# Filter blocks of the convolution two per PE session, and their writes behind the first expert's F tiles

## The chip, the cores and the metric

The kernel runs on one core of a Trainium2 chip. The metric is the device time of one execution in microseconds (us). PE is TensorE, DVE is VectorE, ACT is ScalarE, POOL is GpSimd, SP is SyncE, which here only issues transfers.

## The reference

Two branches of the same 2048 x 512 input x are mixed row by row with a gate:

```python
g = sigmoid((x * gate_w).sum(-1, keepdims=True))
a = x * (long_conv(kv, ssm_k) + kv * ssm_D)    # kv = shift_conv(k) * v
b = top-2-of-8 mixture of experts: sum_e gate_e * ((silu(x@w_gate_e) * (x@w_up_e)) @ w_down_e)
return g * a + (1 - g) * b
```

The long convolution is over 2048 positions for each of 512 channels and is done by a discrete Fourier transform of length 4096, split into two stages for each of the inputs. The experts have F = 1376, that is 11 F tiles of up to 128 rows.

## The kernel before

**The experts.** Their order is found on the chip, the busiest first; each takes up to CAPS rows (568 for the first). `up(ft)` works on one F tile: it loads `raw` (512 KB, gate and up weights, three buffers) and `rd` (256 KB, down weights, two buffers) through SP, splits each into a rounded high part and a low part (`gh` and `dh` on ACT, `gl` and `dl` on DVE), and multiplies: for each half of the rows (h = 0 of 256 columns, h = 1 of 312 for the first expert) twelve matmuls into a PSUM tile `g` and twelve into `u`. These share three PSUM banks. ACT takes silu of `g` into `sg`, which frees the bank of `g`; DVE multiplies `sg` by `u`, which frees the bank of `u`; `hh` (ACT) and `hl` (DVE) split the result. `down` multiplies three or more F tiles' results by `dh`, `dl` into PSUM tiles `yp` (tag "y", three banks).

**The routing.** While the first expert runs, DVE also works out which rows go to the other experts: one-hot tables `hots`, then `vals`, and PE gathers them into lists with 32 small matmuls each (`list`). The rows of the next expert are then gathered by POOL (`xg`), turned on PE (`xgp`) and split into `xh` (ACT) and `xl` (DVE).

**The filter.** Its first stage takes 16 blocks of 128 rows (`ssk`), in the order 1 to 15 and then 0, through four matmuls of 64 rows by 128 columns in full float32 (`c1`); the result goes out to `kd` in device memory, 512 KB a block, and is read back by the filter's second stage (`x_stage2`), much later. The first ten blocks (ks1 to ks10) run in the opening stage, whose order is written out by hand. Their results wait in SBUF: ks2, ks4, ks6 in buffers "ev" (three), ks7 to ks10 in "B" (five), ks1, ks3, ks5 in "A" (six). Writes of ks2, ks4, ks6, ks7 and ks8 (`now`) are issued by POOL as soon as the first expert's last rows are split (anchor "act rest"); the nine other transfers (`rest_k`, which ends with a load of the constant `cr`) follow three per F tile from F tile K0 = 4 on, each behind the ACT split `gh` of that tile (anchor "gh 0 ft").

**The last six blocks** (ks11 to ks15 and ks0) are generators in the list `fill`. `tick()` starts the next entry and advances those that run; it is called in proportion to the F tiles done, `total * seen / n_up` with n_up = 88 * 0.97 = 85.4 and total = 75 entries. After the six filter blocks come the 16 blocks of the input's first stage (`x_stage1`), the 16 steps of the second stage (`x_stage2`) and the four of the last (`y_stage`). Pairs of blocks are loaded by `k_pair`, the first of them (`kr11`) still in the opening stage. Block 0 has the vector `dD` added by POOL. The tile scheduler then decides where in each engine's queue a step's instructions stand.

**A session.** A group of full float32 matmuls between the experts' matmuls is called a session here. `all_free` makes the first matmul of a session wait until the two PSUM banks of tag "m" and the three of tag "y" have been read, so that the rest need no wait.

Of the kernel before, what the change touches and what calls it, by code (L numbers as in the profile page):

```python
# [18 lines left out]
AF = mybir.ActivationFunctionType  # L19
# [11 lines left out]
PL = S // P  # L31
# [23 lines left out]
BUB = (1, 1, 3)  # L55
XG = 3
Z0, Z1 = (7, 6)
RM = 5
K0, LATE = (4, 3)
SEQ_N = 10  # L60
BUSY = (17, 1, 2, 1, 1)
VD = (1, 2, 3, 4, 5, 6)
# [78 lines left out]
def gated_mix(ctx: ExitStack, tc: tile.TileContext, a, out):  # L141
    nc = tc.nc
    sync, act, dve, pool, pe = nc.sync, nc.scalar, nc.vector, nc.gpsimd, nc.tensor
# [7 lines left out]
    kd = dram.tile([P, 2, PL, D], F32, name="kd")  # L151
# [24 lines left out]
    def banks(name):  # L176
        return ps.tile([P, 2 * D], F32, tag="m", bufs=1, name=name)

    def turned(name):
        return ps.tile([P, D], F32, tag="y", bufs=3, name=name)  # L180
# [4 lines left out]
    c1 = cp.tile([P, P], F32, name="c1")  # L185
# [6 lines left out]
    def two(tag, name):  # L192
        return fp.tile([P, 2 * D], F32, tag=tag, bufs={"B": BW, "ev": EV}[tag], name=name)

    def half(t, n):
        return t[:, n * D:(n + 1) * D]

    def split2(t):
        return t.rearrange("p (n d) -> p n d", n=2)
# [24 lines left out]
    def fetch(r, src):  # L224
        with after("sp"):
            d = sync.dma_start(r, src)

        return d

    def load(tag, bufs, name, src):  # L230
        r = t2k(tag, bufs, name)
        fetch(r, src)
        return r


    @contextmanager
    def behind(first):
        with tc.high_priority(), tc.issue_after(first):
            yield
# [9 lines left out]
    written = []  # L249
# [60 lines left out]
    kr = {}  # L310

    k_order = [*range(1, PL), 0]
# [12 lines left out]
    def k_out(pl, **how):  # L325
        return stage1_f32(kr[pl], kd, pl, f"ks{pl}", **how)

    def k_pair(n):
        pl, after_ = k_order[n:n + 2]
        if after_ == pl + 1:  # L330
            w = two("B", f"kr{pl}")
            d = fetch(split2(w), a["ssk"][pl * P:(pl + 2) * P].rearrange("(b p) d -> p b d", b=2))
            kr[pl], kr[after_] = half(w, 0), half(w, 1)
            return d
        k_load(pl)
        k_load(after_)

    def k_stage1(pl):
        n = k_order.index(pl)
        if n % 2 == 0 and pl not in kr:  # L340
            k_pair(n)
        yield
        yield
        k_out(pl)

    krows = {}

# [5 lines left out]
    def x_stage1(pl):  # L353
        if pl == 0:
            with after("sp"):
                sync.dma_start(sk, a["sk"].unsqueeze(0).to_broadcast([P, TAPS, D]))
        for r in range(-3, 1):
            krow(pl + r)
        v = load("T", 3, f"v{pl}", rows(a["v"], pl))
        yield  # L360
        acc = half(two("B", f"acc{pl}"), 0)
        tmp = t2k("T", 3, f"tmp{pl}")
        dve.tensor_mul(acc, krow(pl), sk[:, 0])
        for tap in range(1, TAPS):
            dve.tensor_mul(tmp, krow(pl - tap), sk[:, tap])
            dve.tensor_add(acc, acc, tmp)
        dve.tensor_mul(acc, acc, v)
        hl = pairs(acc, f"xs{pl}", (dve, dve))
        yield
        stage1(hl, xd, pl, f"xs{pl}")  # L370
# [8 lines left out]
    read_y = []  # L379

    def all_free(i, *ready):
        both_free(i)
        for f in (*read_y[-3:], *ready):
            tc.add_manual_dep(i, f.name, mybir.DependencyInfo(
                mybir.DependencyClass.Sync, mybir.DependencyReason.DATA), reason="all at once")
# [12 lines left out]
    def halves(p):  # L398
        return [half(p, n) for n in range(2)]
# [54 lines left out]
    def y_stage(pl):  # L454
# [13 lines left out]
        for n in (0, 2):  # L468
# [8 lines left out]
        yield  # L477

    wait = lambda n: [iter(()) for _ in range(n)]
    fill = ([k_stage1(i) for i in k_order[SEQ_N:]] + wait(BUB[0]) + [x_stage1(i) for i in range(PL)] + wait(BUB[1]) +  # L480
            [g for i in range(NK // 2) for g in (x_stage2(i), iter(()))] + wait(BUB[2]) +
            [g for i in range(0, PL, 4) for g in (y_stage(i), *wait(3))])
    fill.reverse()
# [11 lines left out]
    def after(engine):  # L495
        return nullcontext() if ordered or engine not in anchor else tc.issue_after(anchor[engine])


    def behind_rows(i, name="act rest"):
        tc.add_manual_dep(i, anchor[name].name, mybir.DependencyInfo(  # L500
            mybir.DependencyClass.Sync, mybir.DependencyReason.DATA), reason="behind the gather")
# [443 lines left out]
    for i in range(4):  # L945
        dve.tensor_tensor(hot0[:, i], u0[:, 4 * i:4 * i + 4].unsqueeze(1).to_broadcast([P, P, 4]), io4, op=ALU.is_equal)
        for j in range(4):
            n = 4 * i + j
# [24 lines left out]
    act.activation(sg0, key[:, :1], AF.Silu)  # L973
    behind_rows(first.load_down(0).ins, "act 1")
    behind_rows(first.load_down(1).ins, "act 1")
    behind_rows(k_pair(SEQ_N).ins, "act 1")
    behind_rows(first.load(2), "act 1")
    behind_rows(first.load(3), "act 1")
    evict8()
# [10 lines left out]
    first.product(0, 0, 1, between=last_rows)  # L990
    first.product(0, 1, 0, hi_first=True)
    first.split(1, act, dve)
    now = [f for f in written if f.home == "ev"] + [f for f in written if f.home == "B"][:2]
    for f in now:
        behind_rows(f.write().ins)
    rest_k = [f for f in written if f not in now]
    rest_k.append(SimpleNamespace(write=lambda: pool.dma_start(cr, a["c_r"])))
    order.close()
    ordered = False
# [156 lines left out]
    with tc.For_i(0, nb_v, 1) as b:  # L1156
        with tc.tile_pool(name="over", bufs=1) as op:
            e = nc.values_load(blk[0:1, ds(b, 1)], engines=(mybir.EngineType.SP,),
                               min_val=0, max_val=E - 1)
# [7 lines left out]
            p = turned("oxp").rearrange("p (k n) -> p k n", k=KT)  # L1167
# [5 lines left out]
            for ft, (f0, fw) in enumerate(FT):  # L1173
                n = 2 * KT * fw
# [68 lines left out]
```

## Time and profile before

| | us |
|---|---|
| median of three runs (945.50, 945.69, 954.07) | 945.69 |
| the profiled execution | 943.48 |
| span of its profile | 941.70 |
| outside the span (943.48 - 941.70) | 1.78 |
| PE busy, share of the span | 926.2, 98% |
| DVE busy, share of the span | 642.3, 68% |

A busy PE is not PE at its peak, because matmuls are pipelined and their ends are modelled: in the timeline the start of one matmul to the start of the next is the measure, and a step longer than the usual one shows what lies between. A timeline row has the start in us, the duration in us, engine, line, operation, out<-in, sizes, a count where equal rows are merged, and in brackets the idle time of that engine before it and what ended it. Lines 202 to 204 are the helper that records every expert matmul, so tiles are told apart by name and time.

### The profile page before, as it was taken

To read this page: it belongs to the slowest core of one execution; us is meant where nothing else is said; L and a number is where in the kernel's file an instruction comes from. 1 tells how busy PE (TensorE), PEld (TensorE's weight loads), DVE (VectorE), ACT (ScalarE), POOL (GpSimd) and SP (SyncE) were. 2 spreads that over 40 slices of the span, in tenths; PEclk is the share of its full clock that TensorE was granted. 3 is DMA by queue.
4 is the path that set the end of the run, shared out by engine and by line. 5 is a ranking of instruction groups with operands and counts; after the bars stand their busy time and mean duration, and the time that the engine had idled before them with its cause. 6 is when DMAs were issued, how large, how long until landed. Compare 5 with 4: busy or idle time off the path is not lost.

```text
span 941.7 us, 18495 instructions
## 1 busy us (share of the span) xinstructions
PE 926.2 (98%) x7117; PEld 832.4 (88%) x7117; DVE 642.3 (68%) x1190; ACT 510.2 (54%) x883; POOL 152.1 (16%) x137
## 2 busy tenths in 40 slices
PE   8999999999999999999999999999999999999996
PEld 4789999999999999978898889888887989889984
DVE  4797699999998556556767666765777645553541
ACT  4644344754456545478656876668766544234330
POOL 0333000310003020130101211013010310121012
PEclk9999999999999999999999999999999999999998
DMA  9996945764457463456445655356543786777233
GB/s 331 325 318 203 377 164 179 207 205 155 145 196 195 157 204 111 136 146 201 146 136 169 165 179 179 142 164 176 182 168 123 189 276 180 195 202 212 73 54 46
DMA packets 76381, 172.06 MB, mean 183 GB/s; under 512 B 8481, under 2 KB 9377, under 8 KB 76162
## 3 DMA queue, kind: packets, MB, share of 16 engines
q1 hardware_dynamic: 53490, 121.89, 38.3%
q0 software_dynamic: 12464, 29.02, 13.7%
q10 hardware_dynamic: 10336, 19.93, 5.7%
q8 instruction: 58, 0.95, 0.4%
q14 instruction: 33, 0.27, 0.1%
HBM read 127.24 MB, written 43.57 MB: 181 GB/s over the span
## 4 chain that ended last, share of the span: by engine, by line
PE 87%; issue 4%; ACT 3%; DVE 2%; DMA 2%; POOL 0%; SPq 0%; ACTq 0%; POOLq 0%; DVEq 0%
PE yp L202 9%; PE yp L204 9%; PE yp L203 9%; PE u L202 8%; PE u L203 8%; PE u L204 8%; PE g L202 8%; PE g L203 8%; PE g L204 8%; PE xgp L522 2%; PE zp L392 2%; PE yp L464 2%; PE x2p L392 1%; PE k2p L392 1%; PE yt L716 1%
## 5 line engine op out<-in xcount | busy, mean ns | idle before, releaser
L202 PE MATMUL u<-xh,gh 128*128 128x256 f32 (+14 forms) x704 | 202.6, 288 | 2.4 <-ACT sg L644 2.2
L203 PE MATMUL u<-xl,gh 128*128 128x256 f32 (+14 forms) x704 | 201.1, 286 | 0.0
L204 PE MATMUL u<-xh,gl 128*128 128x256 f32 (+14 forms) x704 | 201.1, 286 | 0.0
L202 PE MATMUL g<-xh,gh 128*128 128x256 f32 (+17 forms) x696 | 201.0, 289 | 0.0
L204 PE MATMUL g<-xh,gl 128*128 128x256 f32 (+17 forms) x696 | 198.9, 286 | 0.0
L203 PE MATMUL g<-xl,gh 128*128 128x256 f32 (+17 forms) x696 | 198.7, 285 | 0.0
L202 PEld LDWEIGHTS u<-xh,gh 128*128 128x128 f32 (+1 forms) x704 | 131.0, 186 | 6.1 <-ACT sg L644 3.0
L202 PEld LDWEIGHTS g<-xh,gh 128*128 128x128 f32 (+1 forms) x696 | 129.5, 186 | 7.7 <-DVE sg L645 1.6
L203 PEld LDWEIGHTS u<-xl,gh 128*128 128x128 f32 (+1 forms) x704 | 131.0, 186 | 3.5 <-issue 3.2
L204 PEld LDWEIGHTS g<-xh,gl 128*128 128x128 f32 (+1 forms) x696 | 129.5, 186 | 4.3 <-issue 4.1
L204 PEld LDWEIGHTS u<-xh,gl 128*128 128x128 f32 (+1 forms) x704 | 131.1, 186 | 0.9 <-issue 0.8
L203 PEld LDWEIGHTS g<-xl,gh 128*128 128x128 f32 (+1 forms) x696 | 129.5, 186 | 2.5 <-issue 0.8
L646 ACT ACTIVATE hh<-sg 128x256 fp32r<-128x256 f32 (+14 forms) x176 | 73.0, 418 | 103.2 <-DVE sg L645 101.5
L202 PE MATMUL yp<-hh,dh 128*128 128x264 f32 (+13 forms) x440 | 127.4, 290 | 0.0
L203 PE MATMUL yp<-hl,dh 128*128 128x264 f32 (+13 forms) x440 | 126.9, 288 | 0.0
L204 PE MATMUL yp<-hh,dl 128*128 128x264 f32 (+13 forms) x440 | 126.5, 288 | 0.0
L644 ACT ACTIVATE sg<-g 128x256 f32<-128x256 f32 (+14 forms) x176 | 68.1, 388 | 98.9 <-PE g L204 96.9
L592 DVE TENSOR_TENSOR gl<-raw,gh 128x1024 fp32r<-128x1024 f32 (+1 forms) x88 | 105.4, 1197 | 19.7 <-ACT gh L586 19.3
L645 DVE TENSOR_TENSOR sg<-sg,u 128x256 f32<-128x256 f32 (+14 forms) x176 | 74.8, 426 | 64.6 <-PE u L204 63.3
L586 ACT ACTIVATE gh<-raw 128x1024 fp32r<-128x1024 f32 (+1 forms) x88 | 91.4, 1038 | 49.2 <-PE u L203 47.5
L513 POOL DMA_INDIRECT xg<-in_q,gidx x37 | 43.9, 1187 | 304.4 <-PE xgp L522 254.0
L653 ACT ACTIVATE dh<-rd 128x512 fp32r<-128x512 f32 (+1 forms) x88 | 53.5, 628 | 71.4 <-PE yp L203 25.5
(289 smaller groups left out, 1609.5 us busy)
## 6 DMA issues: line engine op xcount, KB each, us to landing
raw<-in_wgu SPq DMA_DIRECT2D x80, 512.0 KB, 4.5
rd<-in_wd SPq DMA_DIRECT2D x80, 256.0 KB, 4.5
kl<-kd SPq DMA_DIRECT2D x16, 512.0 KB, 5.3
xl<-xd SPq DMA_DIRECT2D x32, 256.0 KB, 3.8
zd<-ze ACTq DMA_DIRECT2D x16, 512.0 KB, 4.7
zl<-zd SPq DMA_DIRECT2D x16, 512.0 KB, 5.6
out<-zt SPq DMA_DIRECT2D x21, 256.0 KB, 6.4
krow<-in_kpad SPq DMA_DIRECT2D x19, 256.0 KB, 4.4
```

The costliest lines, as they stand in the source:

```text
L202: pe.matmul(p, wh, hi, start=start, stop=False)
L203: pe.matmul(p, wh, lo, start=False, stop=False)
L204: return pe.matmul(p, wl, hi, start=False, stop=stop)
L392: i = pe.matmul(p[r][64 * c:64 * c + 64], w[64 * r:64 * r + 64, 64 * c:64 * c + 64], rows_(r, c)[64 * r:64 * r + 64], start=True, stop=Tru ...
L464: i = pe.matmul(p[b][64 * t:64 * t + 64], c2, half(r[b], t), start=True, stop=True).ins
L513: anchor["pool"] = pool.indirect_dma_start(out=xg[:w], out_offset=None, in_=a["q"], in_offset=bass.IndirectOffsetOnAxis(ap=gidx[:w, col:co ...
L586: anchor[f"gh {r} {ft}"] = act.activation(st["gh", ft], raw, AF.Copy).ins
L592: dve.tensor_sub(st["gl", ft][:, c], raw[:, c], st["gh", ft][:, c].bitcast(F32))
L644: act.activation(sg[:fw, :nn], pp[0][:fw, :nn], AF.Silu)
L645: dve.tensor_mul(sg[:fw, :nn], sg[:fw, :nn], pp[1][:fw, :nn])
L646: act.activation(hh[:fw, sl], sg[:fw, :nn], AF.Copy)
L653: act.activation(dh[:fw], rd[:fw], AF.Copy)
```

## The change

Three things are changed. First, `k_stage1` takes two blocks at a time: one generator loads the pair, and two ticks later one session of eight matmuls does both. The second block goes to two banks of tag "y", and ACT evicts it in two halves. Second, the pair of ks11 and ks12 is no longer loaded in the opening stage, and `fill` begins with K_WAIT = 3 empty entries; each session is followed by an empty one, so the list has 78 entries instead of 75 and `x_stage1` begins three entries later. Third, no write of a block is issued at once: the five that were go to the head of `rest_k`, which now has 14 entries and starts at F tile K0 = 2.

```diff
@@ -56,7 +56,7 @@
 XG = 3
 Z0, Z1 = (7, 6)
 RM = 5
-K0, LATE = (4, 3)
+K0, LATE, K_WAIT = (2, 3, 3)
 SEQ_N = 10
 BUSY = (17, 1, 2, 1, 1)
 VD = (1, 2, 3, 4, 5, 6)
@@ -335,13 +335,25 @@
         k_load(pl)
         k_load(after_)
 
-    def k_stage1(pl):
-        n = k_order.index(pl)
-        if n % 2 == 0 and pl not in kr:
-            k_pair(n)
+    def k_stage1(n):
+        k_pair(n)
         yield
         yield
-        k_out(pl)
+        pls = k_order[n:n + 2]
+        both, p1 = banks(f"ks{pls[0]}p"), [turned(f"ks{pls[1]}p{t}") for t in range(2)]
+        last = None
+        for p, pl in ((halves(both), pls[0]), (p1, pls[1])):
+            for t in (1, 0):
+                part = slice(64 * t, 64 * t + 64)
+                with after("pe") if last is None else behind(last):
+                    i = pe.matmul(p[t], c1[part], kr[pl][part], start=True, stop=True).ins
+                if last is None:
+                    all_free(i)
+                last = i
+        out1(both, kd, pls[0], f"ks{pls[0]}")
+        ev = two("ev", f"ks{pls[1]}e")
+        read_y.extend(act.activation(half(ev, t), p1[t], AF.Copy).ins for t in range(2))
+        act.dma_start(kd[:, :, pls[1], :], split2(ev))
 
     krows = {}
 
@@ -477,7 +489,7 @@
         yield
 
     wait = lambda n: [iter(()) for _ in range(n)]
-    fill = ([k_stage1(i) for i in k_order[SEQ_N:]] + wait(BUB[0]) + [x_stage1(i) for i in range(PL)] + wait(BUB[1]) +
+    fill = (wait(K_WAIT) + [g for n in range(SEQ_N, PL, 2) for g in (k_stage1(n), iter(()))] + wait(BUB[0]) + [x_stage1(i) for i in range(PL)] + wait(BUB[1]) +
             [g for i in range(NK // 2) for g in (x_stage2(i), iter(()))] + wait(BUB[2]) +
             [g for i in range(0, PL, 4) for g in (y_stage(i), *wait(3))])
     fill.reverse()
@@ -973,7 +985,6 @@
     act.activation(sg0, key[:, :1], AF.Silu)
     behind_rows(first.load_down(0).ins, "act 1")
     behind_rows(first.load_down(1).ins, "act 1")
-    behind_rows(k_pair(SEQ_N).ins, "act 1")
     behind_rows(first.load(2), "act 1")
     behind_rows(first.load(3), "act 1")
     evict8()
@@ -990,10 +1001,8 @@
     first.product(0, 0, 1, between=last_rows)
     first.product(0, 1, 0, hi_first=True)
     first.split(1, act, dve)
-    now = [f for f in written if f.home == "ev"] + [f for f in written if f.home == "B"][:2]
-    for f in now:
-        behind_rows(f.write().ins)
-    rest_k = [f for f in written if f not in now]
+    rest_k = [f for f in written if f.home == "ev"] + [f for f in written if f.home == "B"][:2]
+    rest_k += [f for f in written if f not in rest_k]
     rest_k.append(SimpleNamespace(write=lambda: pool.dma_start(cr, a["c_r"])))
     order.close()
     ordered = False
```

On PE the first of the six single sessions stood at the end of the first expert's F tile 0. The names are the product's letter, F tile and half (`u_0_1` is `u` of F tile 0, half 1) with a buffer number behind. Before:

```order
L203 MATMUL u_0_1_586<-xl_435,gh_0_432 128x312
L204 MATMUL u_0_1_586<-xh_434,gl_0_456 128x312
L295 MATMUL ks11p<-kr_482,c_90 128x512 x2
L202 MATMUL g_1_0_644<-xh_434,gh_1_561 128x256
L203 MATMUL g_1_0_644<-xl_435,gh_1_561 128x256
```

After the change the first session of two stands at the end of F tile 9, ahead of a turn of the second expert's rows:

```order
L203 MATMUL u_9_1_1858<-xl_435,gh_9_1808 128x312
L204 MATMUL u_9_1_1858<-xh_434,gl_9_1810 128x312
L349 MATMUL ks11p<-kr_1235,c_90 128x512 x2
L349 MATMUL ks12p_1587<-kr_1235,c_90 128x512
L349 MATMUL ks12p_1586<-kr_1235,c_90 128x512
L534 MATMUL xgp_1_1682<-ident,xg_1_1363 128x128 x4
L202 MATMUL g_10_0_1991<-xh_434,gh_10_1985 96x256
```

ks11 and ks12 moved from F tiles 0 and 1 to F tile 9; ks13 and ks14 stand in F tile 10, and ks15 with ks0 in the second expert. On PE F tiles 1 to 5 of the first expert now follow each other with nothing between them.

On DVE, in F tiles 3 and 4 of the first expert, the product `sg_3_1` stood behind five `vals` before:

```order
L645 TENSOR_TENSOR sg_3_0_930<-sg_3_0_930,u_3_0_917 128x256
L901 TENSOR_TENSOR vals<-hots,pay 128x32x14
L1058 TENSOR_TENSOR pay<-s_150,pay 128x32
L901 TENSOR_TENSOR vals<-hots,pay 128x32x14
L647 TENSOR_TENSOR hl_2_782<-sg_2_1_840,hh_2_781 128x312
L1074 TENSOR_TENSOR pay<-s_150,pay 128x32
L901 TENSOR_TENSOR vals<-hots,pay 128x32x14
L1080 TENSOR_REDUCE s_150<-s_149 128x32
L901 TENSOR_TENSOR vals<-hots,pay 128x32x14
L647 TENSOR_TENSOR hl_3_903<-sg_3_0_930,hh_3_902 128x256
L901 TENSOR_TENSOR vals<-hots,pay 128x32x14
L645 TENSOR_TENSOR sg_3_1_961<-sg_3_1_961,u_3_1_948 128x312
```

It now follows the `hots`, and the `vals` come after it:

```order
L1095 TENSOR_TENSOR hots<-row,rc 128x1024
L1066 CAST pay<-s_150 128x32
L1095 TENSOR_TENSOR hots<-row,rc 128x1024 x2
L910 TENSOR_TENSOR hots<-colf,late 128x448
L657 TENSOR_TENSOR sg_3_1_957<-sg_3_1_957,u_3_1_944 128x312
L1082 CAST pay<-s_150 128x32
L604 TENSOR_TENSOR gl_5_1241<-raw_5_1237,gh_5_1239 128x1024
L1067 TENSOR_TENSOR pay<-s_150,pay 128x32
L657 TENSOR_TENSOR sg_4_0_1144<-sg_4_0_1144,u_4_0_1131 128x256
L913 TENSOR_TENSOR vals<-hots,pay 128x32x14 x2
```

`gl_4` stood behind the `hots` before and is ahead of them now, and the five `vals` moved behind `sg_3_1`. The `list` on PE that reads them moved from the middle of `u_4_0` to the end of `g_6_0`.

At the start of the second expert the last two turns of its rows stood well ahead of the product that needs them before (`xgp_3` nine matmuls, `xgp_4` a whole product ahead); now PE goes straight from them to the half that needs them:

```order
L204 MATMUL yp_2_3_256_1959<-hh_8_1701,dl_8_1768 128x312
L534 MATMUL xgp_3_1970<-ident,xg_3_1680 128x128 x4
L534 MATMUL xgp_4_2059<-ident,xg_4_1771 128x44 x4
L202 MATMUL g_0_1_2132<-xh_1359,gh_0_2095 128x276
L202 MATMUL u_0_1_2145<-xh_1359,gh_0_2095 128x276
L202 MATMUL g_1_0_2249<-xh_1359,gh_1_2243 128x280
```

What moved is `xgp_3` and `xgp_4`, from F tile 10 of the first expert to between two products of the second, where `g_0_1` reads what ACT makes of them.

## Rows read from the trace of the kernel before

**Rows 1.** The page: shares of the span, by engine, of the chain of work that ended last.

```profile
PE 87%; issue 4%; ACT 3%; DVE 2%; DMA 2%; POOL 0%; SPq 0%; ACTq 0%; POOLq 0%; DVEq 0%
```

**Rows 2.** Stretches of ten us in the first expert: busy time of each engine with instruction count, the granted TensorE clock, the busy share of the DMA engines and their GB/s.

```profile
40.00:50.00 10.00, 10.00 (x74) 8.92 (x73) 7.23 (x28) 4.68 (x8) 0.00 (x0) 1.00 1.03 377
...
60.00:70.00 10.00, 9.45 (x88) 8.13 (x87) 10.00 (x23) 4.83 (x8) 5.00 (x7) 1.00 0.89 329
```

**Rows 3.** Timeline of PE around the first (ks11) and the last (ks0, between 72.06 and 73.35) of the six sessions of one block, and the list behind it.

```profile
38.00 0.31 PE L203 MATMUL u<-xl,gh 128*128 128x312 f32 x1
38.15 0.30 PE L204 MATMUL u<-xh,gl 128*128 128x312 f32 x1
38.38 1.13 PE L295 MATMUL ks11p<-kr,c 64*128 64x512 f32 x4
39.44 0.39 PE L202 MATMUL g<-xh,gh 128*128 128x256 f32 x1
39.66 0.27 PE L203 MATMUL g<-xl,gh 128*128 128x256 f32 x1
...
72.06 0.30 PE L204 MATMUL u<-xh,gl 128*128 128x312 f32 x1
...
73.35 1.25 PE L909 MATMUL list<-vals,hots 128*128 128x70 bf16 x32
74.43 0.36 PE L202 MATMUL yp<-hh,dh 128*128 128x256 f32 x1
```

**Rows 4.** Timeline of PE where two float32 jobs stand back to back: ks7 and ks8 of the opening stage, with ks9 alone behind them (`none` is a filler), and two jobs of the second stage (`zp` and `k2p`) between expert matmuls.

```profile
24.62 1.13 PE L295 MATMUL ks7p<-kr,c 64*128 64x512 f32 x4 [0.33 <-ACT ks5e L268]
25.59 1.02 PE L295 MATMUL ks8p<-kr,c 64*128 64x512 f32 x4
26.54 0.28 PE L809 MATMUL none<-ones 128*128 128x256 bf16 x1
...
27.67 1.13 PE L295 MATMUL ks9p<-kr,c 64*128 64x512 f32 x4
28.73 0.28 PE L809 MATMUL none<-ones 128*128 128x256 bf16 x1
...
656.66 0.28 PE L203 MATMUL g<-xl,gh 128*128 128x256 f32 x1
656.87 1.09 PE L392 MATMUL zp<-y,mi 64*64 64x512 f32 x8
657.78 1.04 PE L392 MATMUL k2p<-kl,mf 64*64 64x512 f32 x8
658.75 0.39 PE L204 MATMUL g<-xh,gl 128*128 128x256 f32 x1
```

**Rows 5.** Timeline of PE in the first expert: the last matmul of `g_3_1` and the first of `u_3_1`; the two matmuls of `u_4_0` between which the list of 32 stands; the first of `u_4_1`.

```profile
60.65 0.30 PE L204 MATMUL g<-xh,gl 128*128 128x312 f32 x1
61.09 0.41 PE L202 MATMUL u<-xh,gh 128*128 128x312 f32 x1
...
66.68 0.28 PE L202 MATMUL u<-xh,gh 128*128 128x256 f32 x1
...
68.44 0.37 PE L203 MATMUL u<-xl,gh 128*128 128x256 f32 x1
...
70.48 0.30 PE L202 MATMUL u<-xh,gh 128*128 128x312 f32 x1
```

**Rows 6.** Timeline of DVE in the same stretch: `gl_2`, `dl_2`, `sg_2_1`, the first of the five `vals`, and `sg_3_1`.

```profile
40.04 1.22 DVE L592 TENSOR_TENSOR gl<-raw,gh 128x1024 fp32r<-128x1024 f32 x1
...
46.86 0.69 DVE L655 TENSOR_TENSOR dl<-rd,dh 128x512 fp32r<-128x512 f32 x1 [2.63 <-ACT dh L653]
...
60.57 0.46 DVE L645 TENSOR_TENSOR sg<-sg,u 128x312 f32<-128x312 f32 x1
...
63.31 0.61 DVE L901 TENSOR_TENSOR vals<-hots,pay 128x448 bf16<-128x448 bf16 x1
...
67.25 0.46 DVE L645 TENSOR_TENSOR sg<-sg,u 128x312 f32<-128x312 f32 x1
```

**Rows 7.** Timelines of POOL, ACT and SP: the first early write, the split `gh_2`, the issue of `rd_2`, and its split `dh_2`.

```profile
34.90 0.77 POOL L272 DMA_DIRECT2D kd<-ks2e  x1 [5.77 <-ACT xh L524]
...
38.34 1.06 ACT L586 ACTIVATE gh<-raw 128x1024 fp32r<-128x1024 f32 x1 [1.15 <-PE u L203]
...
38.58 0.33 SPq L622 DMA_DIRECT2D rd<-in_wd  x1
...
46.19 0.63 ACT L653 ACTIVATE dh<-rd 128x512 fp32r<-128x512 f32 x1 [2.69 <-DMA rd<-in_wd]
```

**Rows 8.** Timeline of PE in the opening stage: a turn of rows, and the first product that reads ACT's split of it.

```profile
28.85 0.60 PE L522 MATMUL xgp<-ident,xg 128*128 128x128 f32 x4
...
30.44 0.74 PE L606 MATMUL g<-xh,gh 128*128 128x256 f32 x4
```

**Rows 9.** Timeline of PE: the longest wait of the later stages.

```profile
408.56 0.39 PE L202 MATMUL u<-xh,gh 128*128 128x264 f32 x1 [1.36 <-ACT sg L644]
```

**Rows 10.** Timelines of POOL, SP and PE: the addition of `dD` to block 0, the issue of `rd_9` (the loads of blocks 15 and 0 now stand ahead of it on SP), and the turn `xgp_4` of the second expert's rows.

```profile
57.17 4.63 POOL L323 TENSOR_TENSOR kr<-kr,dD 1x512 f32<-1x512 f32 x1 [18.64 <-DMA kr<-in_ssk]
...
98.24 0.44 SPq L625 DMA_DIRECT2D rd<-in_wd  x1
...
146.36 0.44 PE L522 MATMUL xgp<-ident,xg 44*128 44x44 f32 x4
```

## The prediction

> **What bounds the kernel now.** I read the page first: the chain of work that ended last is 87% PE, 3% ACT and 2% DMA [rows 1]. Then the stretches: in the first expert, where the change acts, PE is busy 10.00 of 10 us at a granted clock of 1.00, while the DMA engines are full (share 1.03 at 377 GB/s) and later DVE is too (10.00 of 10) [rows 2]. So three things could bound this stretch, and a busy share does not say which. The timeline of PE does: from one matmul's start to the next is about 0.145 us for 312 columns (38.00 to 38.15) and, by the columns, 0.12 for 256. Longer steps are what can be won. I find three kinds: the sessions of the filter [rows 3], a few waits for DVE [rows 5], and waits for ACT much later, the longest 1.36 us [rows 9]. On PE no wait for a transfer stands in the stretch; transfers are felt one engine further back, where ACT waits 2.69 us for `rd_2` and DVE 2.63 us for ACT [rows 6, 7], and PE does not stop for it. PE's own work is therefore the bound, and a saving there reaches the end one for one as long as DVE keeps up.
>
> **The six single sessions.** ks11: the last matmul before it starts at 38.15, the next after it at 39.44, that is 1.29 us, of which 0.145 belongs to the former: 1.15. The first expert matmul behind it takes 0.22 to the next start instead of 0.12: another 0.10. One session costs 1.25 us. ks0 reads the same, 72.06 to 73.35 [rows 3]. Six make 7.50 us, all of it on PE.
>
> **The three sessions of two.** None stands between expert matmuls before, so I bound the second block. ks7 with ks8 takes 24.62 to 26.54, 1.92 us up to the filler; ks9 alone 27.67 to 28.73, 1.06. The second block adds 0.86 [rows 4]. The later pair of jobs `zp` and `k2p` takes 656.66 to 658.75, 2.09 less 0.12, plus the same 0.10: 2.07 in all, which says 0.82 [rows 4]. The upper bound is a block that streams for the 1.06 of ks9. I take 0.86, the same kind of block: 1.25 + 0.86 = 2.11 a session, 6.33 for three. Bounds: 3 x 2.07 = 6.21 and 3 x 2.31 = 6.93. So the edit on PE is worth 7.50 - 6.33 = **1.17 us**, between 0.57 and 1.29. The eviction of the second block in two halves is ACT work in place of one; ACT is busy 4.68 to 4.83 of 10 us [rows 2] and covers it.
>
> **Where the sessions are no longer.** F tiles 1 to 5 lose five sessions, 5 x 1.25 = 6.25 us of PE time in which DVE could catch up. The waits of before there are `u_3_1`, 60.65 to 61.09, 0.44 less 0.145 = 0.30 (it follows `sg_2_1`, which ends at 60.57 + 0.46 = 61.03 [rows 6]), and the list in `u_4_0`: 66.68 to 68.44 is 1.76, less 0.12, less the 1.08 of a list that does not wait (73.35 to 74.43 [rows 3]): 0.56. The list is moved behind, so these 0.86 us go. Next to be late is `u_4_1`: by what held `u_3_1`, it needs `sg_3_1`. PE would reach it at 70.48 - 6.25 - 0.30 - (1.76 - 0.12) = 62.3, since the list has left. DVE: from `gl_2` at 40.04 to `sg_3_1` at 67.25 are 27.21 us [rows 6]. The five `vals`, 5 x 0.6 = 3.0, now come later, and the 2.63 idle goes if `rd_2` lands earlier. Then `sg_3_1` starts at 40.04 + 27.21 - 3.0 - 2.63 = 61.6 and ends at 62.1, 0.2 us before PE wants it. I cost this place at nothing, but its cover is only 0.2 us: each further us that DVE idles costs PE one.
>
> **A new wait.** At the second expert's start PE goes from `xgp_4` directly to `g_0_1`, which reads ACT's split. In the opening stage a turn starts at 28.85 and ends at 29.45; the product that reads it starts at 30.44, 1.0 us later [rows 8]. Before, `xgp_4` had a product between. I charge 1.0; below it lies 0, if ACT is quick, above it 2.7, the wait of ACT for a late `rd` in its queue [rows 7]. So waits are 0.86 off and 1.0 on: 0.1 worse.
>
> **Loads and writes.** The early load `kr11` leaves the opening stage and the five early writes leave 34.90; no PE wait hung on them, so they count nothing directly. The writes now wait for `gh_2`, which ends at 38.34 + 1.06 = 39.40 [rows 7]: three of them start only 4.5 us later than the first did, 0.8 after `rd_2` is issued (38.58). The waiting instructions stand on POOL; behind them there are only other block writes, `cr` and the gathers for the second expert, first needed at its turns, far later. The writes on ACT's queue of ks11 to ks0 come later too; the second stage reads them after hundreds of us.
>
> **Later stages.** 78 entries instead of 75 over the same 85.4 F tiles: the same instructions, `x_stage1` three entries later. The waits there (1.36 the longest [rows 9]) may fall away or come anew; I take 0, and plus or minus 2 for the range.
>
> **Sum.** 943.48 - 1.17 + 0.1 = 942.4 for an execution like the profiled one. The median shown is 945.69, 2.21 above it, so on its scale 945.69 - 1.1 = **944.6**. About 1% (9.5 us) is what a measurement of this kernel can tell from no change, so this forecast is "same".
>
> **Rivals.** (a) DVE lags: PE gives its lead back at `u_4_1` and after. For it speaks DVE at 10.00 of 10 [rows 2] and the cover of 0.2 us; against it the room DVE has later and the order that puts `gl_4` and `gl_5` early. At worst all 6.25 us return: 944.6 + 6.25 = 950.9; half of it 947.7. It is slower than before, from the point where DVE idles more than 1.3 us ahead of `sg_3_1` (0.2 of cover and the 1.1 gained).
>
> (b) The writes are not out of the way: `rd_2` and `rd_3` meet the writes released at 39.40 as they met them before, and DVE's 2.63 us stay. Then `sg_3_1` ends at 64.7, PE waits 64.7 - 62.3 = 2.4, and the time is 947.0. For it: DMA share 1.03 [rows 2], and 0.8 us of lead against a landing that took 46.19 - 38.58 = 7.6 us [rows 7]. Against: `rd_2` now goes first, with `kr11` and five writes less ahead of it. The Trainium skill, DMA: Bandwidth & Descriptors, section "Issuing engines are not separate DMA queues", speaks for (b): transfers issued from any engine run on the same 16 DMA engines and interleave, so a write released on POOL slows a load from SP that is under way. The trace agrees that POOL's writes and SP's loads were slow together.
>
> (c) The waits go and none comes: 944.6 - 1.0, and up to 2 of the later ones: 941.6 to 943.6.
>
> (d) PE stands in front of a session. `all_free` waits for all five banks, and the last session also for block 0, whose addition on POOL waited 18.64 us for its load and took 4.63 [rows 10]. If it is not there when PE comes, all later work is late; slower by over 1% needs 9.5 + 1.1 = 10.6 us. Against: the loads of 15 and 0 stand ahead of `rd_9`, issued at 98.24, and `xgp_4`, after which the session comes, ran at 146.36 [rows 10]: 48 us of room.
>
> **How the numbers follow.** My forecast (943 to 946) 0.55, (a) 0.14, (b) 0.13, (c) 0.13, (d) 0.04, and 0.01 for a gain I do not see. The range holds the forecast, (c), (b) and the first half of (a): 941.0 to 948.5. Faster by over 1% would take 9.5 us, and all that could go is 1.29 + 0.86 + some 2: 0.01. Slower by over 1% is (d), and little of (a): 0.05. Within 1%: 0.94.
>
> **What would show it.** Right: three steps of some 2.1 us over the usual at ks11, ks13 and ks15 and none in F tiles 1 to 5; ACT's wait for `rd_2` under 1 us; `u_4_1` at about 62.3; a step of about 1 us behind `xgp_4`. Wrong: a pair over 2.5 us (no saving); waits on DVE in F tiles 3 to 6 of together more than 2 us, or `dh_2` still at 46 ((a) or (b)); PE idle just before a session (d). What would make the forecast wrong without these is a later stage whose order came out with other waits.

## The result, and the profile after

The changed kernel takes 954.65 us (median of ten runs, 953.30 to 961.05) against 945.38 of the kernel before in the same session (ten runs, 943.97 to 954.07): a ratio of 1.0099, 95% interval 1.0074 to 1.0125. It is 1% slower. The prediction was 944.6, from 941.0 to 948.5; the time lies outside. Whatever the kernel, some executions take about 9 us longer than most (954.07 here; three of the six of pairs_pool below, its profiled one among them), so a ratio, which is worked out from the single executions, can differ from the quotient of two medians.

The profiled execution took 953.69, its span 951.9, that is 10.2 more than before (941.7). PE does the same 7117 matmuls. Its busy time is 2.9 us more (929.1 against 926.2), its idle time 7.3 more. The page's groups of expert matmuls show where PE idles: ahead of the last bar is the busy time and mean, behind it the idle time in front of them and what ended most of it. Before:

```profile
L202 PE MATMUL u<-xh,gh 128*128 128x256 f32 (+14 forms) x704 | 202.6, 288 | 2.4 <-ACT sg L644 2.2
...
L202 PE MATMUL g<-xh,gh 128*128 128x256 f32 (+17 forms) x696 | 201.0, 289 | 0.0
...
L202 PE MATMUL yp<-hh,dh 128*128 128x264 f32 (+13 forms) x440 | 127.4, 290 | 0.0
```

After:

```profile
L202 PE MATMUL u<-xh,gh 128*128 128x256 f32 (+14 forms) x704 | 202.4, 287 | 3.6 <-ACT sg L656 3.6
L202 PE MATMUL g<-xh,gh 128*128 128x256 f32 (+17 forms) x696 | 200.7, 288 | 3.8 <-ACT xh L536 3.0
...
L202 PE MATMUL yp<-hh,dh 128*128 128x264 f32 (+13 forms) x440 | 127.8, 292 | 2.3 <-DVE ya L694 1.1
```

The idle time in front of these three groups was 2.4 and became 9.7, which is the whole of the 7.3. To see at what time, I went through PE's timeline of both and added up what every step between expert matmuls takes over the usual by more than 0.15 us (a step with other work in it is compared with the same work elsewhere). All later tables give these **waits** by stretch:

| stretch | before | after |
|---|---|---|
| 40 to 125 us, first expert | 1.0 | 2.1 |
| 125 to 170, its end and the second expert's start | 0 | 5.9 |
| 170 to 400 | 0 | 0.7 |
| 400 to 800, filter's second stage | 2.7 | 4.5 |
| sum | 3.7 | 13.2 |

The 9.5 more, 0.3 of a later first product (30.72 against 30.44 in [rows 8]) and about 1.0 in small steps, less about 0.6 for the other work between the expert's matmuls (the sessions' gain among it), make the 10.2. So over half of the loss stands in one place, at 125 to 170 us. PE's waits there, by what ended them (us in total, times, longest; this idle time adds up to 5.2, and the 5.9 also holds the slower steps beside it):

```profile
PE g L202 <- ACT xh L536: 2.5, 1, 2.5
PE yp L202 <- DVE ya L694: 1.1, 2, 0.8
PE u L202 <- ACT sg L656: 0.9, 1, 0.9
PE yp L202 <- ACT ks14e L355: 0.7, 1, 0.7
```

Five waits of four kinds, on two engines. ACT's timeline, from the eviction of the first session on (a row ACTq is a transfer that ACT issues itself):

```profile
124.33 1.00 ACT L255 ACTIVATE ks11e<-ks11p 128x1024 f32<-128x1024 f32 x1
125.23 0.59 ACT L355 ACTIVATE ks12e<-ks12p 128x512 f32<-128x512 f32 x1
129.20 0.58 ACTq L256 DMA_DIRECT2D kd<-ks11e  x1
129.83 0.60 ACT L355 ACTIVATE ks12e<-ks12p 128x512 f32<-128x512 f32 x1 [4.00 <-PE u L204]
130.32 0.59 ACT L536 ACTIVATE xh<-xgp 128x512 fp32r<-128x512 f32 x1
...
131.04 0.38 ACT L656 ACTIVATE sg<-g 96x256 f32<-96x256 f32 x1
...
137.78 0.60 ACT L355 ACTIVATE ks14e<-ks14p 128x512 f32<-128x512 f32 x1 [2.21 <-DMA kd<-ks11e]
...
149.86 1.28 ACT L218 ACTIVATE xs<-acc 64x512 fp32r<-64x512 f32 x2 [6.70 <-DVE acc L379]
...
152.55 0.78 ACT L536 ACTIVATE xh<-xgp 128x512 fp32r<-128x512 f32 x2
```

From 125.82 to 129.20 ACT does nothing: next in its queue is the write of ks11, whose data have been ready since 125.33. (The bracket of the row at 129.83 names `u`, which was long done.) Behind it stand `xh` and the silu that PE waits for (0.9). Later ACT stands for the landing of that same write, since two of the three "ev" buffers belong to a session (0.7), and then 6.70 us for DVE, with `xh` of xgp_3 and xgp_4 behind it (2.5). What the write waited for, the listing of the two queues shows (row number, line, transfer, the semaphores that it waits for; rows 122 to 132 are SP's, then two of ACT's and one of SP's):

```
122 L368 DMA sk<-in_sk 128x2048 [waits DMAHW5_49]
123 L226 DMA krow_2334<-in_kpad 128x512 [waits DMAHW6_49,DMASW2_49]
125 L637 DMA rd_1_2311<-in_wd 128x512 [waits DMAHW7_49,DMAHW1_49,DVE_49]
126 L226 DMA krow_2336<-in_kpad 128x512 [waits DMAHW0_49,DMASW3_49]
...
132 L226 DMA krow_2444<-in_kpad 128x512 [waits DMAHW5_49,DMASW6_49]
123 L256 DMA kd<-ks11e 256x1x512 [waits DMAHW6_49,Activation_49]
126 L356 DMA kd<-ks12e 256x1x512 [waits DMAHW7_49,Activation_49]
133 L226 DMA v_2446<-in_v 128x512 [waits DMAHW0_49,Pool_49]
```

In this program transfers of SP and ACT use eight semaphores DMAHW0 to 7 in turn, and one that takes a semaphore waits until its last user has landed. For the write of ks11 that is a `krow` of `x_stage1`, issued at 121.08 into full DMA engines. The stretches (columns as in [rows 2]) show two more things: the DMA engines are full from 120 to 130, and DVE is full from 140 to 150. The granted clock is 1.00 in all of them, so it has no part in this loss:

```profile
120.00:130.00 10.00, 10.00 (x71) 8.58 (x70) 3.79 (x8) 4.35 (x8) 2.34 (x3) 1.00 1.00 376
130.00:140.00 10.00, 8.46 (x54) 6.52 (x53) 8.28 (x14) 5.90 (x11) 0.00 (x0) 1.00 0.87 315
140.00:150.00 10.00, 9.18 (x70) 8.96 (x70) 9.90 (x20) 1.94 (x5) 0.00 (x0) 1.00 0.18 69
```

The sessions themselves cost what was forecast. ks13 with ks14, in PE's timeline:

```profile
132.97 0.31 PE L203 MATMUL u<-xl,gh 128*96 128x312 f32 x1
133.21 1.13 PE L349 MATMUL ks13p<-kr,c 64*128 64x512 f32 x4
134.17 1.02 PE L349 MATMUL ks14p<-kr,c 64*128 64x512 f32 x4
135.12 0.39 PE L202 MATMUL yp<-hh,dh 128*128 128x256 f32 x1
135.34 0.28 PE L203 MATMUL yp<-hl,dh 128*128 128x256 f32 x1
```

135.12 - 132.97 - 0.145 = 2.01, and 0.10 for the slow first one behind it: 2.11, as in the prediction.

### The profile page after: what moved, and what is told of

It is laid out like the page before. It is cut to its first block, busy times and chain, and to the rows that moved or that the text cites. A ratio compares the mean times of both kernels' runs of the same rounds, so it can differ in the third digit from the quotient of the medians.

```text
span 951.9 us, 18470 instructions
## 1 busy us (share of the span) xinstructions
PE 929.1 (98%) x7117; PEld 833.7 (88%) x7117; DVE 643.2 (68%) x1190; ACT 508.9 (53%) x886; POOL 145.1 (15%) x137
## 5 line engine op out<-in xcount | busy, mean ns | idle before, releaser
L667 DVE TENSOR_TENSOR dl<-rd,dh 128x512 fp32r<-128x512 f32 (+1 forms) x88 | 59.7, 686 | 52.4 <-ACT dh L665 52.1
```

Source lines behind the costliest of these rows:

```text
L667: dve.tensor_sub(dl[:fw], rd[:fw], dh[:fw].bitcast(F32))
```

## The experiments

Fifteen kernels were timed, each with a profile. One table holds all results; a ratio is to the kernel before in the same session, with its 95% interval (the medians of the kernel before were 944.34 to 945.38). The waits of PE are those of the table above, by stretch of the profiled execution; those of pairs_pool, whose first product came 9.9 us late, are taken 9.9 us later. In some kernels PE ran at a lower granted clock behind a wait, and the slower steps are in these sums too. The profile's list of idle times alone gives, from 125 to 170, 5.2 in the changed kernel, 8.2 in pool_writes (clock 0.66 from 140 to 150), 5.4 in pairs_late (0.86 from 150 to 160) and 4.8 in loads_ahead_pool (0.83 from 130 to 150).

| kernel | median us | ratio (interval) | span | 40-125 | 125-170 | 170-400 | 400-800 |
|---|---|---|---|---|---|---|---|
| before | 945.38 | 1 | 941.7 | 1.0 | 0 | 0 | 2.7 |
| changed | 954.65 | 1.0099 (1.0074, 1.0125) | 951.9 | 2.1 | 5.9 | 0.7 | 4.5 |
| pool_writes | 959.41 | 1.0146 (1.0112, 1.0180) | 958.3 | 2.4 | 9.6 | 0 | 5.7 |
| pairs_late | 955.58 | 1.0124 (1.0087, 1.0161) | 953.6 | 3.0 | 6.8 | 0 | 3.8 |
| late_writes | 947.75 | 1.0045 (1.0012, 1.0077) | 945.0 | 4.0 | 0 | 0.5 | 3.0 |
| singles_late | 948.65 | 1.0033 (1.0010, 1.0056) | 946.9 | 0.9 | 0 | 1.1 | 5.5 |
| sessions_earlier | 956.52 | 1.0153 (1.0108, 1.0199) | 952.5 | 5.3 | 0.8 | 2.2 | 4.0 |
| after_75 | 960.69 | 1.0174 (1.0145, 1.0202) | 957.1 | 9.2 | 0.8 | 1.3 | 3.0 |
| pairs_only | 961.18 | 1.0162 (1.0139, 1.0185) | 960.4 | 11.4 | 1.6 | 1.1 | 3.0 |
| writes_ahead | 955.08 | 1.0102 (1.0081, 1.0123) | 956.0 | 4.1 | 5.6 | 0 | 4.3 |
| loads_ahead | 954.50 | 1.0077 (1.0037, 1.0117) | 951.2 | 2.6 | 4.0 | 1.6 | 3.8 |
| pairs_pool | 960.25 | 1.0116 (1.0048, 1.0183) | 962.4 | 5.8 | 1.3 | 0.7 | 3.0 |
| x1_later | 960.33 | 1.0148 (1.0086, 1.0210) | 958.9 | 1.7 | 6.1 | 4.6 | 5.3 |
| loads_ahead_pool | 957.92 | 1.0102 (1.0039, 1.0165) | 955.1 | 2.9 | 7.6 | 0 | 4.0 |
| x1_much_later | 948.88 | 1.0051 (1.0015, 1.0087) | 945.0 | 1.7 | 0.7 | 0.5 | 4.2 |
| earlier_pool | 955.93 | 1.0116 (1.0070, 1.0163) | 950.8 | 2.0 | 0.5 | 2.1 | 5.8 |
| before_pool | 946.90 | 1.0017 (0.9983, 1.0051) | 943.9 | 2.2 | 0 | 0.3 | 2.7 |

**First round: one part at a time.** The first theory (A) was the one that the profile suggests: ACT stands in front of its own writes. Its rivals were the put-off writes (B) and the spacing of 78 entries (C).

pool_writes, the writes of ks11 to ks0 by POOL (the second blocks' too):

```diff
-            act.dma_start(dst[:, :, pl, :], split2(both))
+            (pool if dst is kd else act).dma_start(dst[:, :, pl, :], split2(both))
```

> The changed kernel, but the writes of ks11 to ks0 are issued by POOL and no longer by ACT. Theory A (ACT): in the changed kernel the write of ks11 stands in ACT's queue from 125.8 to 129.2 us, in the middle of the loads for the input's first stage, and the silu, the turns and the evictions behind it are late; the waits of PE at 131.5, 138.4, 145.1 and the 2.74 us at 153.4 come from there. Then these 5.2 us go and the time is 954.65 - 5 = about 949.5. Theory B (writes): the 14 writes put off to F tile 2 are what costs; then the time stays at 954 to 955. Theory C (spacing): 78 entries in place of 75 put the later stages where PE waits more; also 954 to 955.

Measured 959.41, slower still. ACT no longer stands (`sg` 127.41 in place of 131.04), but now DVE does, for a load of x_stage1, and `ya`, which frees the bank that PE wants, stands behind it in DVE's queue. DVE's timeline:

```profile
136.56 0.69 DVE L377 TENSOR_TENSOR tmp<-krow,sk 128x512 f32<-128x512 f32 x1 [6.77 <-DMA krow<-in_kpad]
```

PE's waits from 120 to 170 (columns as above):

```profile
PE yp L202 <- DVE ya L694: 6.0, 1, 6.0
PE g L202 <- ACT xh L536: 2.2, 1, 2.2
```

So ACT's stand was true and not the whole: taken away, the wait moved on, and the one behind xgp_3 and xgp_4 stayed (2.2). The Trainium skill says in DMA: Bandwidth & Descriptors, section "Issuing engines are not separate DMA queues", that transfers of all engines share the 16 DMA engines and interleave, and that issuing from several engines only saves the sequencer's time to start a transfer, usually small beside the transfer. The first half agrees with this run (issued by POOL 3.3 us earlier, the writes met the krow loads at a DMA share of 1.03 from 130 to 140). On the second, the issue itself took 0.58 us of ACT's queue, which agrees; but the wait in front of an issue, which that sentence does not count, was 3.4 us on ACT in the changed kernel, and 11.4 in pairs_only below.

pairs_late is the changed kernel with the five early writes of before and

```diff
-K0, LATE, K_WAIT = (2, 3, 3)
+K0, LATE, K_WAIT = (4, 3, 3)
```

late_writes is the kernel before with the change's `rest_k` (no write at once) and

```diff
-K0, LATE = (4, 3)
+K0, LATE = (2, 3)
```

singles_late is the kernel before with

```diff
-    fill = ([k_stage1(i) for i in k_order[SEQ_N:]] ...
+    fill = (wait(3) + [k_stage1(i) for i in k_order[SEQ_N:]] ...
...
-    behind_rows(k_pair(SEQ_N).ins, "act 1")
```

> The changed kernel with the early writes of before: five issued at once, nine from F tile 4 on; sessions of two and the three empty entries stay. Theory A: nothing near 125 to 155 us changes, 954 (+-1). Theory B: the writes were the cost, back to about 945. Theory C: 954 (+-1).

> The kernel before with one part of the change: all writes wait for the first expert's F tiles, 14 of them from F tile 2 on. Sessions of one block and 75 entries stay. Theory A: no session lies near 125 us, so 945 (+-1.5). Theory B: 950 or more. Theory C: 945 (+-1.5).

> The kernel before with three empty entries ahead of the list (78 in all) and the load of ks11 and ks12 put off with it; sessions of one block, writes as before. x_stage1 and all that follows stand where the changed kernel has them; ks11 to ks15 stand in F tiles 3 to 8, only ks0 near 130 us. Theory A: most of the loss is gone, 946 to 949. Theory B: 945. Theory C: the later stages cost what they cost in the changed kernel, 951 to 955.

Measured 955.58, 947.75 and 948.65. The put-off writes are not the cause (pairs_late keeps the loss, against theory B); alone they cost 3 to 4 us, because single sessions behind F tiles 1 and 2 then wait 1.5 for an eviction and 2.0 for a load. The 78 entries cost 3 to 4 us with sessions of one, with no wait at 125 to 170, and 5.5 in place of 2.7 in the second stage. So 948.65 lies where theory A put it (946 to 949) and below theory C's 951 to 955: the spacing is a part of the loss, and the smaller one.

**Second round: sessions and writes moved.** sessions_earlier is the changed kernel with both of these lines, after_75 with the first alone:

```diff
-K0, LATE, K_WAIT = (2, 3, 3)
+K0, LATE, K_WAIT = (2, 3, 0)
-BUB = (1, 1, 3)
+BUB = (4, 1, 3)
```

pairs_only is the kernel before with the new `k_stage1` (its first pair still loaded early) and

```diff
-    fill = ([k_stage1(i) for i in k_order[SEQ_N:]] ...
+    fill = ([g for n in range(SEQ_N, PL, 2) for g in (k_stage1(n), iter(()))] ...
```

writes_ahead is the changed kernel without the writes of these six blocks' results; in their place POOL writes the loaded blocks, long before, so that `kd` holds other values:

```diff
         k_pair(n)
+        for q in k_order[n:n + 2]:
+            for t in range(2):
+                pool.dma_start(kd[:, t, q, :], kr[q])
...
-        act.dma_start(kd[:, :, pls[1], :], split2(ev))
```

> The changed kernel with its three empty entries behind the sessions and no longer ahead of them: still 78 entries and every later stage in its place, but the three sessions now stand in F tiles 7 to 9 (about 90 to 115 us), ahead of x_stage1's loads. Theory A2 (crowd): the loss near 125 to 165 us, 5.9 us of waits, comes from the session's writes (3 MB) meeting x_stage1's loads and the second expert's tiles; which queue issues them only decides who stands behind, ACT in the changed kernel, DVE when POOL issued them. Then these waits go here: 954.65 - 5 = 949 to 950, and what is left over 944.3 is the spacing of the 78 entries. Theory C2: x_stage1 itself, three entries later and closer together, makes this crowd; the time stays at 953 to 955.

> The changed kernel without the three empty entries (K_WAIT = 0, 75 entries): sessions in F tiles 7 to 9, x_stage1 and the second stage where the kernel before has them; the writes stay put off. Theory A2 with the spacing as second cause: 944.3 - 1.1 (pairs) + 0 to 3 (put-off writes) = 943 to 946.5. If the pairs themselves cost the time: 950 or more.

> The kernel before with sessions of two alone: 75 entries, first pair loaded early, five writes at once, nine from F tile 4. Theory A2: 944.3 - 1.1 = 943.2, if no wait comes anew. If pairs cost by themselves: 950 or more.

> The changed kernel with the results of ks11 to ks0 not written; in their place POOL writes the loaded blocks themselves (as many bytes to the same places) as soon as they are loaded, 40 to 105 us, so kd holds other values. Sessions, loads and all later work stand as in the changed kernel. Theory A2: without 3 MB of writes between 125 and 165 us the waits there go, 949 to 950. Theory C2: they stay, 953 to 955.

Measured 956.52, 960.69, 961.18 and 955.08. Theory A2 falls as it was put: with the last block write issued at 110 us and none on ACT, the waits at 125 to 170 stay (writes_ahead, 5.6), for `ya` on DVE and for an `xh` behind an `xs` that waited 6.85 for DVE. With the sessions elsewhere they go (0.8), so theory C2 falls too: x_stage1 alone does not make them, nor does it in singles_late, where it stands at the same place (0). But the time did not fall, because PE now waited at 110 to 120 us for the second half of ks14, 2.7 in sessions_earlier and more with 75 entries, 7.0 in after_75 and 7.8 in pairs_only. pairs_only shows it bare. ACT's timeline:

```profile
104.30 1.02 ACT L255 ACTIVATE ks13e<-ks13p 128x1024 f32<-128x1024 f32 x1 [0.50 <-PE ks13p L350]
105.24 0.60 ACT L356 ACTIVATE ks14e<-ks14p 128x512 f32<-128x512 f32 x1
117.20 0.52 ACTq L256 DMA_DIRECT2D kd<-ks13e  x1
117.83 1.06 ACT L599 ACTIVATE gh<-raw 128x1024 fp32r<-128x1024 f32 x1 [11.99 <-DMA krow<-in_kpad]
```

SP's timeline:

```profile
110.57 2.76 SPq L226 DMA_DIRECT2D krow<-in_kpad  x4
```

The stretches:

```profile
110.00:120.00 10.00, 2.18 (x17) 1.98 (x16) 1.09 (x1) 1.89 (x3) 0.00 (x0) 0.69 1.03 386
120.00:130.00 10.00, 10.00 (x64) 10.00 (x65) 5.67 (x13) 1.50 (x3) 0.00 (x0) 0.79 0.54 208
```

ACT is ready to write ks13 at 105.8 and issues it at 117.20, held by a `krow` that SP issues only at 110.57 (the listing has DMAHW7 on both). PE stands 7.8 us for the second half of `ks14e` behind it, and then runs at a granted clock of 0.79. The sessions stand so late although the list has no empty entries: in the order on PE, ks11 and ks12 come behind the third list, after F tile 6. That the two banks of tag "y" are the reason is likely, but no run shows it.

**Third round: is it the order?** Theory O: x_stage1's steps and the sessions stand together in the in-order queues of ACT and DVE, ahead of work that PE needs, and each has a late transfer to wait for. loads_ahead is the changed kernel with the loads of `sk` and four `krow` taken out of `x_stage1(0)` into a generator `x_rows`, in the empty entry behind ks13 and ks14:

```diff
-    ... for g in (k_stage1(n), iter(()))] ...
+    ... for g in (k_stage1(n), x_rows() if n == SEQ_N + 2 else iter(()))] ...
```

loads_ahead_pool adds the edit of pool_writes; pairs_pool is pairs_only with that edit; x1_later is the changed kernel with

```diff
-BUB = (1, 1, 3)
+BUB = (2, 1, 2)
```

> The changed kernel; the first loads of x_stage1 (sk and four rows krow, 2 MB) are issued two entries earlier, in the empty entry behind ks13 and ks14, its computing where it was. Theory O (order in the queues): the sessions and x_stage1 now stand together at the second expert's start; on ACT the write of ks11 waits for a load of x_stage1 to land, on ACT and DVE x_stage1's steps, late with their loads, stand ahead of evictions, xh and ya that PE needs. With the loads landed before, 3 to 5 of the 5.9 us near 130 to 165 us go: 950 to 952. Theory T (the traffic alone): as many bytes, only spread, so they go too, and the DMA engines are no longer full from 120 to 140. Theory D (DVE and ACT have too much work there): 954 to 955.

> The kernel with sessions of two alone (961.18), the writes of ks11 to ks0 issued by POOL. There ACT stood 12 us in front of the write of ks13, until a load of x_stage1 that SP issued 5 us later had landed, and PE stood 8 us and then ran at a granted clock of 0.69 and 0.79. Theory O: these 8 us and some 4 of the clock go: 946 to 950. Otherwise, if the sessions of two themselves cost it: above 955.

> The changed kernel with x_stage1 (and the second stage) one entry later, still 78 entries. On ACT the second xs of x_stage1 no longer stands ahead of xh from xgp_3; the sessions and their writes are where they were. Theory O: the 2.74 us behind xgp_3 and xgp_4 shrink to about 1 and the wait for ya (0.87) goes, so 951 to 953. If the writes or the sessions alone are the cause: 954 to 955 and the waits stay.

> x_stage1's first loads two entries earlier and the writes of ks11 to ks0 issued by POOL. With POOL alone the wait went from ACT to DVE, which stood 6.8 us for krow. Theory O: now neither has one to wait for: 948 to 951. Theory D: 954 or more.

Measured 954.50, 960.25, 960.33 and 957.92. In loads_ahead ACT issues the write of ks11 at once (126.48 behind 126.34), which confirms what held it, but 4.0 of the 5.9 us are still there, now mainly for `sg` and `ya` on DVE, although the DMA share from 130 to 140 fell from 0.87 to 0.39: that speaks against theory T, and 954.50 is where theory D put it. But the test was not complete. Only the first four rows `krow` were ahead; the fifth, issued at 123.81, still held DVE, with the `sg` behind it for which PE waited 1.1; DVE's timeline:

```profile
131.15 0.69 DVE L375 TENSOR_TENSOR acc<-krow,sk 128x512 f32<-128x512 f32 x1 [1.33 <-DMA krow<-in_kpad]
...
133.91 0.42 DVE L664 TENSOR_TENSOR sg<-sg,u 96x256 f32<-96x256 f32 x1
```

The gain against the changed kernel lies within the intervals. pairs_pool: the 7.8 us are gone (5.8 in place of 11.4 in that stretch); ACT's timeline:

```profile
114.37 0.59 ACT L356 ACTIVATE ks14e<-ks14p 128x512 f32<-128x512 f32 x1
116.58 1.06 ACT L599 ACTIVATE gh<-raw 128x1024 fp32r<-128x1024 f32 x1 [1.61 <-DMA raw<-in_wgu]
```

But 2.1 of the 5.8 are new. As in pool_writes the same loads now held DVE, with the `ya` behind that PE waited for; DVE's timeline:

```profile
130.11 0.69 DVE L378 TENSOR_TENSOR tmp<-krow,sk 128x512 f32<-128x512 f32 x1 [5.23 <-DMA krow<-in_kpad]
```

Its profiled execution began its first product at 40.34 and not at 30.44, in an opening at half the clock (last section); without these 9.9 its span is 952.5 against 960.4. So theory O's 946 to 950 was not reached, neither by that nor by the median. In x1_later the wait behind xgp_3 and xgp_4 fell from 2.5 to 0.5, as the order on ACT says, but `ya` on DVE rose to 3.4 and the eviction of ks14 to 1.4, and two waits for DVE's product came new at 205 and 219 us (3.7): theory O's total was wrong there. loads_ahead_pool still had 4.8 us of idle time (2.5 for `sg`, 1.4 for `ya`) and the lower clock. Its time is against theory O's 948 to 951, its trace is not against the mechanism: DVE stood 2.52 us ahead of that `sg` for the fifth `krow`, issued at 125.46 and landed at 133.51 (the bracket of its row names the write of ks12, which landed only at 136.62). So these two runs do not tell theory O from a DVE with too much to do at once.

**Fourth round: the meeting from the other side.** x1_much_later is the changed kernel with

```diff
-BUB = (1, 1, 3)
+BUB = (5, 1, 1)
```

earlier_pool is sessions_earlier with the edit of pool_writes, before_pool the kernel before with it.

> The changed kernel with x_stage1 four entries on (80 entries in all, so later stages move too): the sessions and their writes stay at the second expert's start, x_stage1's first blocks go to F tile 7 of the second expert. If the meeting of the two makes the 5.9 us of waits between 125 and 170 us, they shrink to 1.5 or less (about 0.6 behind xgp_3 and xgp_4), whatever the later stages then cost; if the sessions or their writes alone make them, 4 us or more stay. The time as a whole can be higher, since all later stages have other places: 950 to 960.

> The changed kernel with the three sessions ahead of x_stage1 (F tiles 7 to 9) and their writes issued by POOL. If the 2.88 us of PE at 110.31 were ACT in front of a write, they go: 956.5 - 3 = 953 to 954. If they were something else: 956 to 957.

> The kernel before, the writes of ks11 to ks0 issued by POOL and no longer by ACT. If a write on ACT costs wherever it stands: 1 to 3 us faster, 942 to 944. If only its place among the loads of 105 to 130 us matters: 944 to 946, no difference.

x1_much_later has the sessions where the changed kernel has them, with their writes on ACT, and takes 948.88. By the medians 5.8 us of the 9.3 are back, by the ratios about half (1.0051 against 1.0099; the intervals overlap by 0.0013), by the profiled spans 6.9 of 10.2. From 125 to 170 PE's waits are 0.7, where 1.5 or less was expected if the meeting makes them. DVE is busy 18.3 us from 120 to 160, in the changed kernel 27.6. PE's waits there:

```profile
PE g L202 <- ACT xh L536: 0.4, 1, 0.4
```

ACT's timeline at the write of ks11:

```profile
124.94 0.59 ACT L355 ACTIVATE ks12e<-ks12p 128x512 f32<-128x512 f32 x1
125.07 0.58 ACTq L256 DMA_DIRECT2D kd<-ks11e  x1
125.70 0.60 ACT L355 ACTIVATE ks12e<-ks12p 128x512 f32<-128x512 f32 x1 [0.17 <-ACT ks12e L355]
```

With that the meeting is shown from both sides: sessions moved away from x_stage1, or x_stage1 moved away from the sessions, and the 5.9 us of waits at 125 to 170 go. Only the second also gives time back, since the sessions moved ahead meet other late transfers. earlier_pool: the 2.9 us at 110 go, and the stretch up to 125 falls from 5.3 to 2.0; there ACT had stood for a transfer again. ACT's timeline in sessions_earlier:

```profile
110.74 0.52 ACTq L256 DMA_DIRECT2D kd<-ks13e  x1
111.36 1.06 ACT L598 ACTIVATE gh<-raw 128x1024 fp32r<-128x1024 f32 x1 [5.73 <-DMA out<-zt]
```

The time as a whole does not settle it (955.93 against 956.52, intervals overlap). before_pool: no difference that these runs can tell (0.9983 to 1.0051); in the kernel before, ACT's own writes cost nothing that can be seen where they stand.

## Why the prediction was wrong

**The six single sessions, the three sessions of two.** Right: 2.11 forecast, 2.11 measured for ks13 with ks14, and none between F tiles 1 and 5. The gain of 1.17 us was there, and was an eighth of what else moved. That ACT "covers" the second eviction because it is busy 4.68 to 4.83 of 10 us did not hold: from 120 to 140 it was busy 4.35 and 5.90 of 10, and PE waited for it all the same, because of what stood ahead in its queue.

**Where the sessions are no longer.** Nearly right. PE was ready for `u_4_1` at 62.53 (62.39 + 0.145), forecast 62.3, and waited 0.5:

```profile
62.39 0.30 PE L204 MATMUL g<-xh,gl 128*128 128x312 f32 x1
63.21 0.41 PE L202 MATMUL u<-xh,gh 128*128 128x312 f32 x1 [0.52 <-ACT sg L656]
```

The step took `sg_3_1` on DVE for what is awaited. It ran 1.1 us later than forecast (62.72, forecast 61.6), but the row names ACT: the silu of `g_4_1`, the product just done, which the step did not have. DVE's and ACT's timelines:

```profile
62.72 0.46 DVE L657 TENSOR_TENSOR sg<-sg,u 128x312 f32<-128x312 f32 x1
...
62.73 0.43 ACT L656 ACTIVATE sg<-g 128x312 f32<-128x312 f32 x1 [2.71 <-PE g L204]
```

The waits from 40 to 125 are 1.1 more than before, where 0.9 less was forecast. ACT waited 0.60 for `rd_2`, as said (under 1), but 2.15 for `rd_3`, and the silu behind it cost PE 0.43 over the usual step at 45.30: a small part of rival (b). Rival (a) did not come, nor (d).

**A new wait** is the first step that failed. The place was right and its upper bound, 2.7, near: behind xgp_3 and xgp_4 PE stood 2.5. But I took 1.0, from a turn of the opening stage, and named a late `rd` as the reason for more. ACT's queue there holds, ahead of `xh`, two `xs` of x_stage1, and the second of them waited 6.70 for DVE. And it was not one wait but five, 5.9 us in all, where the step had room for one.

**Later stages** is the second. "78 entries instead of 75: the same instructions, x_stage1 three entries later", cost 0, plus or minus 2. Three entries later, x_stage1 and the sessions meet at the second expert's start, which makes the 5.9; and the second stage's waits rose by 1.8 in the profile. singles_late, with the 78 entries and no pairs, puts the spacing alone at a ratio of 1.0033. Here the words "the same instructions" hid that ACT and DVE work in order, so that another neighbour in the queue is another wait. The last sentence of the signs named this way to be wrong, a later stage whose order came out with other waits, but it was given plus or minus 2 and no rival of its own.

**Loads and writes.** "Count nothing directly" held in the whole (pairs_late). But of the writes of ks11 to ks0 the prediction said only that the second stage reads them much later. It did not ask what stands behind them on ACT: `xh`, the silu and the evictions that free PE's banks.

What stays open: how the 5.9 us divide between ACT's writes, x_stage1's loads and DVE's load of work, since each that was taken away or moved alone left most of the waits or raised them (9.6, 4.0, 5.6, 6.1). Nor was a place of the later stages found that is worth more than the kernel before; no kernel here beats it.

## What to carry to other kernels

An edit that moves work to another place must be read on the in-order engines around its new place, not only on the one whose work it saves: for each row moved in, what it waits for, and what that PE needs stands behind it. A transfer issued from a compute engine's queue is such a row, since the whole engine waits with it, here also for a transfer of another queue that had the same semaphore before it. When one wait is taken away and the time does not fall, look one engine further: here the same late loads held ACT, then DVE.

## What the runs showed of the hardware

In pairs_only, after PE had stood for 7.8 us, the granted clock was 0.69 in the stretch from 110 to 120 and 0.79 in the next, that is partly at the lower of the two levels. In pool_writes it was 0.66 in the stretch where PE's wait of 6.0 us ended:

```profile
140.00:150.00 10.00, 4.69 (x23) 4.69 (x24) 8.95 (x15) 2.12 (x4) 0.00 (x0) 0.66 0.09 38
```

After a shorter wait both came: it was 0.83 from 130 to 150 around the 2.5 us of loads_ahead_pool, and 1.00 from 150 to 170 around the 2.5 us of the changed kernel. A whole opening can run at the lower level: in the profiled execution of pairs_pool PE was busy 7.15 of the first 10 us (7.69 in the kernel before), and then

```profile
10.00:20.00 10.00, 10.00 (x60) 5.45 (x57) 2.78 (x10) 2.98 (x14) 0.00 (x0) 0.50 1.02 373
20.00:30.00 10.00, 9.78 (x52) 5.09 (x53) 5.83 (x22) 2.64 (x9) 0.81 (x2) 0.50 0.42 138
```

the granted clock stayed at 0.50 (1.2 GHz) for these 20 us, with PE busy nearly throughout, and the first product came 9.9 us later than before.
